# Attention and feed-forward: the first chunk's softmax transposed on TensorE, and a new plan of the first stage

## The chip, the cores and the metric

One core of one Trainium2 chip. A time is the device time of one execution in microseconds (us). The kernel is launched once and holds both parts of the computation.

## What is computed

Sliding-window attention over 8 batches and 8 heads, with 576 positions of width 64, and then a feed-forward layer on the result. Heads 0 to 3 see the 32 last positions (plain), heads 4 to 7 every fourth of the last 128 (dilated).

```python
scores = scale * np.matmul(q, k.transpose(0, 1, 3, 2))
rel = pos[:, None] - pos[None, :]
mask_plain = (rel >= 0) & (rel < window)                                  # window = 32
mask_dil = (rel >= 0) & (rel < window * dilation) & (rel % dilation == 0) # dilation = 4
scores = np.where(masks[None, :, :, :], scores, -1000000000.0)
attn = np.exp(scores - np.max(scores, axis=-1, keepdims=True))
attn = attn / (np.sum(attn, axis=-1, keepdims=True) + 1e-09)
x = np.matmul(attn, v)           # then (batch, position) x (head, width): 4608 x 512
h = x @ w_in                     # 512 x 2048
g = 0.5 * h * (1.0 + erf(h * inv_sqrt2))
return g @ w_out                 # 2048 x 512
```

## The kernel before

The 4608 rows are worked on in 9 chunks of 512: chunk c is the first 512 positions of batch c, and the ninth holds the remaining 64 of every batch. Within a chunk the heads go in four pairs: pairs 0 and 1 are plain, 2 and 3 dilated.

The attention of a pair has these steps, which are also the names in the plan. `scores` (line 318): 64 small matmuls of q and k and, in chunks 0 and 1, two with the unit matrix that put the mask into the bank first. `low` (`lowest`): the maximum, on VectorE. `exp` (`softmax`): 8 activations on ScalarE. `sums` and `norm`: the reciprocal of the sums, and the product with it. `t`: the transpose of the softmax. `av`: its product with v. `x` (`xout`): ScalarE copies the result as the rounded high part of x, VectorE subtracts to get the low part.

The feed-forward layer has 16 weights f, each with 512 columns of w_in's and 512 of w_out's work. They lie in memory as 64-bit numbers, and VectorE and ScalarE split each into a high and a low part (`w_split`, from line 235, and `w_high`, line 261). A weight in the list `TWICE` is loaded a second time, shifted by two bytes (`w_load_mid`), which spares VectorE one shift and one combination (lines 244 and 246) for one short instruction (line 242). The first `HALVED` weights are split in two halves. `ffn_h` (line 533) is 12 matmuls for one f, three for each pair's x; then gelu, and g is split like x. `ffn_o` (line 548) is 12 matmuls that add to four banks.

The first stage, up to chunk 0's last product, holds chunk 0's attention, all weights, chunk 1's attention and chunk 0's feed-forward layer. Its order is made on the host by the class `Plan`: each step has costs for its engines, steps it comes after, buffers that it takes and gives back, and a rank; the step that can start earliest goes next. The result is one fixed order of instructions on each engine. `FIRST`, `BLOCK`, `FETCH` and `FETCH_BUSY` are the planner's idea of how TensorE's program is loaded. The order of the loads, all issued by SyncE, is written out in `ORDER`: q and Q are the q and k of chunk 0 and 1, v and V their v, w a weight, m its shifted copy, n a tiny transfer that waits for a pair's sums.

PSUM has eight banks. Chunk 0's scores are in banks 6 and 7 (pairs 0 and 1) and 4 and 5 (pairs 2 and 3), each pair in its half of the columns; its products with v go to banks 0 to 3. The buffer `b67` stands for banks 6 and 7: chunk 0 holds it from pair 0's scores to pair 1's `exp`, then chunk 1 uses it for two pairs at a time: scores, transposes, products with v, until their x is out. `h` stands for banks 4 and 5, which `ffn_h` uses in turn; `ffn_o` adds up in banks 0 to 3.

In chunk 0 the transposes are VectorE's (`turn`, line 419: 32x32 blocks), so that v is needed in blocks of 32 keys, in an array `v_0` of its own with 5 blocks. In chunk 1 TensorE transposes (`turn_pe`, line 431, four of 128x128), ScalarE copies the result out of PSUM (line 434), and `av_one` (line 445) multiplies 64 keys deep.

The steps after the first stage (chunks 1 to 8, with the next chunk's attention between) are in an order written out by hand.

Of the kernel before, what the change touches and what calls it, by code (L numbers as in the profile page):

```python
# [18 lines left out]
P = 128  # L19
N = 512  # L20
REST = S - N
NCH = B + 1
# [11 lines left out]
TWICE = (3, 5, 6, 7, 8, 10, 11, 12, 13, 14)  # L34

HALVED = 3
# [11 lines left out]
RANK = dict(att0=-6760, split=19680, high=-4520, gelu=-6180, o=3550, scores=(-7120, -6830), low=(-5340, -70, -2990,  # L48
            680), exp=(3250, 2670, 3780, 6310), norm=(9560, 7320, 1160, 2270), t=(4820, 2320, 2390, 3790),
            av=(-14470, -8190), x=(-12250, -3790, -5560, -9110), store=5000)  # L50
# [106 lines left out]
def attn_ffn(ctx: ExitStack, tc: tile.TileContext, qk, qk_lp, qk_ld, v_0, v, v_ld, w, outT):  # L157
# [133 lines left out]
    def load_v(s):  # L291

        yield {"DMA": 1.6 if s.c == 0 else 2.6}
        a, b = xs[s.c][s.p], xs[s.c][s.p + 1]
        if s.c == 0:
            t = wpool.tile([P, 2, NU + 1, 2 * D], F32, tag="w", name="v_0")
            src = v_0[s.p // 2]
        else:
            t = wpool.tile([P, 2, NU, 2, 2 * D], F32, tag="w", name="v_sb")
            src = v[s.c - 1, s.p // 2]  # L300
        nc.sync.dma_start(t, src)
        a.v, b.v = t[:, 0], t[:, 1]
        if s.c == 1:
            a.v, b.v = (x.rearrange("p u j d -> p (u j) d").rearrange("p (a r) d -> p a r d", a=2) for x in (a.v, b.v))
# [13 lines left out]
    def scores(s, bank):  # L318

        yield {"PE:132": 1.15}  # L320
        s.at = 0 if s.wide else s.p % 2 * NU * 2 * KB
# [105 lines left out]
    def turn_pe(s, bank):  # L427

        yield {"PE:8": 0.25}
        for i in range(NU):  # L430
            nc.tensor.transpose(ps[:, bank, i * P:(i + 1) * P], s.all[:, 2 * i:2 * i + 2].rearrange("p i k -> p (i k)"), diag.bitcast(F32))
# [4 lines left out]
    def av_one(s, bank):  # L436

        yield {"PE:128": 1.0}
        for a in range(2):
            for r in range(4):  # L440
                for k in range(2):
                    rows = slice(k * 64, k * 64 + 64)
                    c0 = s.p % 2 * 256 + (2 * r + a) * KB
                    for h in range(2):
                        nc.tensor.matmul(ps[h * D:(h + 1) * D, bank + k, c0:c0 + KB], s.v[rows, a, r, h * D:(h + 1) * D],
                                         s.t[rows, h, a, r * KB:(r + 1) * KB], start=True, stop=True)

    def av(s, px, u0=0):

        yield {"PE:156": 0.95}  # L450
        s.px = px
        if s.c == 0:
            tiles = s.t.rearrange("p i j b -> p (i j) b")
            for m in (1, 3, 0, 2, 4):
                for r in range(4):
                    rows = slice(32 * r, 32 * r + 32)
                    if m == 0 and first(s, r, 0):
                        continue
                    for h in range(2):
                        def mm(q, i, start=m == 1):  # L460
                            nc.tensor.matmul(px(r)[h * D:(h + 1) * D, q * KB:(q + i.stop - i.start) * KB if i.step is None else (q + 2) * KB],  # L461
                                             s.v[rows, m, h * D:(h + 1) * D], tiles[rows, i], start=start, stop=m == NU)
                        i = [2 * (h * NU + slot(s, u)) for u in range(NU)]
                        if m == 1 and first(s, r, 0):
                            if s.plain:
                                mm(0, slice(i[0], i[0] + 3, 2))
                            else:
                                mm(0, slice(i[0], i[0] + 1))
                                mm(1, slice(i[1], i[1] + 1), False)
                        elif m == 0:  # L470
                            mm(0, slice(i[0], i[0] + 1))
                        elif m == NU:
                            mm(NU - 1, slice(i[NU - 1] + 1, i[NU - 1] + 2))
                        else:
                            mm(m - 1, slice(i[m - 1] + 1, i[m - 1] + 3))
            return
# [21 lines left out]
    def xout(s, px):  # L498
# [8 lines left out]
        elif s.c == 1:  # L507
            px = ps[:, 6:8, s.p % 2 * 256:s.p % 2 * 256 + 256].rearrange("p k (r a n) -> p k r a n", r=4, a=2)
# [17 lines left out]
    def ffn_h(c, f, gs):  # L526
        yield {"PE:24": 2.73}
        bank = ps[:, 4 + f % 2]
        n = 0
        for cc in range(NC):  # L530
            x = xs[c][cc].x
            for t, xx in ((0, 0), (1, 0), (0, 1)):
                nc.tensor.matmul(bank, weights[f][:, t, cc * P:(cc + 1) * P], x[:, xx],  # L533
                                 start=n == 0, stop=n == 3 * NC - 1)
                n += 1
        yield {"ACT/gelu": 0.6}
# [100 lines left out]
    for p in range(NPAIR):  # L637
        s, k = xs[0][p], (0, p)
        rank, even = RANK["att0"] + 10 * p, p % 2 == 0
# [206 lines left out]
```

## Time and profile before

| | |
|---|---|
| three runs, median | 911.31 us (911.13 to 911.84) |
| the profiled execution, its own time | 910.51 us |
| its span in the profile | 908.4 us |
| granted TensorE clock, mean | 0.985 |
| TensorE (PE) matmuls busy | 873.2 us, 96% |
| weight loads on TensorE (PEld) | 718.9 us, 79% |
| VectorE (DVE) busy | 357.9 us, 39% |
| ScalarE (ACT) busy | 370.9 us, 41% |
| GpSimd (POOL) busy | 9.6 us, 1% |
| read from and written to HBM | 66.06 and 9.44 MB |

The span runs from the first to the last instruction of the profiled execution; its own time is 2.1 us more. Shares are averages over the whole span, and the change touches only the beginning of it, so rows of single stretches say more than the table. A row of a wait gives as its reason what came last before it; "issue" means that nothing that the profile shows was missing.

### The profile page before, as it was taken

The numbers are of one execution on the slowest core, as the hardware profiler recorded it, in microseconds if no ns is written. First come the engines' busy times: TensorE is split into PE (matmuls) and PEld (weight loads), VectorE is DVE, ScalarE is ACT, GpSimd is POOL, SyncE is SP. The second block draws the span as 40 slices with busy tenths as digits, with TensorE's granted clock in tenths as the row PEclk, the third lists the DMA queues.
The fourth block names the chain that finished last, engine by engine and source line by source line (L and its number), as shares of the span: only waits on it lengthen the run. The fifth ranks groups of instructions, "written<-read, shape, count | busy, mean of one in ns | idle before, by whom it ended". The sixth has DMA issues, their size and how long they took to land.

```text
span 908.4 us, 19090 instructions
## 1 busy us (share of the span) xinstructions
PE 873.2 (96%) x8408; PEld 718.9 (79%) x8408; DVE 357.9 (39%) x612; ACT 370.9 (41%) x1016; POOL 9.6 (1%) x48
## 2 busy tenths in 40 slices
PE   4569999999999999999999999999999999999998
PEld 3458887888888888888888888888888888888886
DVE  3699991462146214621263225421552155212020
ACT  5548442543245423632273327232543254414040
POOL 4000000000000000000000000000000000000000
PEclk9599999999999999999999999999999999999999
DMA  9964614200410032003300330024000330010001
GB/s 370 417 252 182 260 63 151 83 0 1 170 65 1 1 129 105 1 1 122 113 1 1 117 118 1 1 79 155 2 0 20 133 144 21 1 38 12 1 1 47
DMA packets 17075, 76.72 MB, mean 84 GB/s; under 512 B 1888, under 2 KB 2144, under 8 KB 12768
## 3 DMA queue, kind: packets, MB, share of 16 engines
q1 hardware_dynamic: 16992, 75.50, 22.3%
q8 instruction: 66, 1.08, 0.5%
q14 instruction: 17, 0.14, 0.0%
HBM read 66.06 MB, written 9.44 MB: 83 GB/s over the span
## 4 chain that ended last, share of the span: by engine, by line
PE 92%; DVE 3%; ACT 2%; issue 1%; DMA 1%; POOL 0%; SPq 0%; POOLq 0%; ACTq 0%
PE ps L548 42%; PE ps L533 42%; PE ps L339 3%; PE ps L491 3%; ACT sm L384 1%; PE ps L461 1%; PE ps L325 1%; DMA raw_qk<-qk 1%; DVE raw_w L250 1%; PE ps L483 0%; DVE x L522 0%; DVE raw_w L246 0%; DVE st L353 0%; DVE weight L256 0%; ACT x L519 0%
## 5 line engine op out<-in xcount | busy, mean ns | idle before, releaser
L533 PE MATMUL ps<-x,weight 128*128 128x512 f32 x1728 | 404.5, 392 | 4.2 <-ACT weight L261 4.2
L548 PE MATMUL ps<-g,weight 128*128 128x512 f32 x1728 | 402.3, 391 | 0.0
L533 PEld LDWEIGHTS ps<-x,weight 128*128 128x128 f32 x1728 | 324.5, 189 | 74.1 <-ACT weight L261 5.2
L548 PEld LDWEIGHTS ps<-g,weight 128*128 128x128 f32 x1728 | 322.7, 188 | 67.4 <-issue 0.2
L543 DVE TENSOR_TENSOR g<-gf,g 128x512 fp32r<-128x512 f32 x144 | 99.6, 691 | 386.3 <-ACT g L541 386.2
L538 ACT ACTIVATE gf<-ps 128x512 f32<-128x512 f32 x144 | 86.1, 598 | 330.2 <-PE ps L533 330.2
L541 ACT CAST g<-gf 128x512 fp32r<-128x512 f32 x144 | 89.4, 621 | 4.6
L384 ACT ACTIVATE sm<-sm,st 128x64 f32<-128x64 f32 (+1 forms) x224 | 74.9, 336 | 0.1
L522 DVE TENSOR_TENSOR x<-ps,x 128x512 fp32r<-128x512 f32 (+1 forms) x40 | 31.8, 812 | 93.0 <-ACT x L519 93.0
L214 ACT COPY o_sb<-ps 128x512 f32<-128x512 f32 (+1 forms) x35 | 20.3, 581 | 108.7 <-PE ps L548 103.2
L519 ACT CAST x<-ps 128x512 fp32r<-128x512 f32 (+1 forms) x40 | 29.5, 768 | 66.4 <-PE ps L491 40.6
L424 DVE STREAM_TRANSPOSE turned<-sm 32x256 f32<-32x256 f32 x104 | 45.4, 436 | 2.0
L384 ACT ACTIVATION_READ_ACCUMULATOR sm<-sm,st 128x1 f32 x224 | 42.1, 188 | 0.0
L339 PEld LDWEIGHTS ps<-raw_qk 64*32 64x32 f32 x2304 | 26.4, 114 | 10.5 <-issue 9.3
L339 PE MATMUL ps<-raw_qk 64*32 64x64 f32 (+1 forms) x2304 | 30.9, 245 | 3.5 <-issue 2.7
L491 PEld LDWEIGHTS ps<-turned,v_sb 64*64 64x64 f32 x1664 | 25.4, 135 | 4.6 <-issue 4.6
L491 PE MATMUL ps<-turned,v_sb 64*64 64x32 f32 x1664 | 26.9, 220 | 0.0
L261 ACT CAST weight<-raw_w 128x1024 fp32r<-128x1024 f32 (+1 forms) x19 | 18.8, 989 | 7.8 <-DVE raw_w L250 7.7
L419 DVE STREAM_TRANSPOSE turned<-sm 128x512 f32<-128x512 f32 x30 | 21.3, 711 | 0.9
L384 ACT ACTIVATE sm<-ps,st 128x64 f32<-128x64 f32 x64 | 19.0, 334 | 6.4 <-PE ps L339 4.6
L406 DVE TENSOR_TENSOR sm<-sm,st 128x512 f32<-128x512 f32 x30 | 20.7, 691 | 0.9
L256 DVE SCALAR_TENSOR_TENSOR weight<-raw_w,spare 128x1024 fp32r<-128x1024 uint32 (+1 forms) x19 | 20.1, 1058 | 0.9
(51 smaller groups left out, 230.9 us busy)
## 6 DMA issues: line engine op xcount, KB each, us to landing
raw_qk<-qk SPq DMA_DIRECT2D x32, 512.0 KB, 6.2
raw_w<-w SPq DMA_DIRECT2D x16, 1024.0 KB, 7.7
v_sb<-v SPq DMA_DIRECT2D x15, 1024.0 KB, 5.1
mid_w<-w SPq DMA_DIRECT2D x10, 1023.5 KB, 8.3
outT<-o_sb SPq DMA_DIRECT2D x35, 256.0 KB, 2.1
raw_qk<-qk_ld SPq DMA_DIRECT2D x2, 1024.0 KB, 7.0
v_wide<-v_ld SPq DMA_DIRECT2D x2, 768.0 KB, 5.8
v<-v SPq DMA_DIRECT2D x2, 640.0 KB, 11.3
```

Of the source, the lines that this page charges most:

```text
L339: nc.tensor.matmul(s.sc[32 * r:32 * r + 32, h, c0:c0 + s.nk], x[:, q0:q0 + 32], x[:, k0:k0 + s.nk], start=s.c > 1, stop=s.c > 1 or u == NU ...
L384: nc.scalar.activation(t, s.sc[:, i // NU, at:at + 2 * KB] if s.c < 2 else t, AF.Exp, bias=s.st[:, 0, i:i + 1], scale=SCALE if s.c < 2 els ...
L419: nc.vector.transpose(s.t.rearrange("p i j b -> p (i j b)"), s.all.rearrange("p i k -> p (i k)"))
L424: nc.vector.transpose(s.t[32 * to:32 * to + 32, :, r % 2], s.all[32 * r:32 * r + 32, :, j * KB:(j + 1) * KB])
L491: nc.tensor.matmul(px(r)[h * D:(h + 1) * D, u * KB:(u + 1) * KB], s.v[rows, u, j, h * D:(h + 1) * D], s.t[rows, h * NU + slot(s, u), j], s ...
L519: nc.scalar.copy(h, y)
L522: nc.vector.tensor_sub(l, y, h)
L533: nc.tensor.matmul(bank, weights[f][:, t, cc * P:(cc + 1) * P], x[:, xx], start=n == 0, stop=n == 3 * NC - 1)
L538: nc.scalar.activation(gf, bank, AF.Gelu)
L541: nc.scalar.copy(g[:, 0], gf)
L543: nc.vector.tensor_sub(g[:, 1], gf, g[:, 0])
L548: nc.tensor.matmul(ps[:, d], weights[f][:, t, DM + d * P:DM + (d + 1) * P], gs[f][:, u], start=f == 0 and n == 0, stop=f == NF - 1 and n == 2)
```

## The change

Chunk 0's attention now goes as chunk 1's does: TensorE transposes the softmax (`turn_pe`), the result is copied out of PSUM by ScalarE or by VectorE as the plan chooses, and `av_early` (the former `av_one`) multiplies 64 keys deep. v of chunk 0 has the layout of the other chunks (1024 KB for two pairs instead of 640). Each pair of chunk 0 has two banks of its own for scores, transposes and products (4 and 5, 0 and 1, 2 and 3, 6 and 7); `b67` is taken by pair 3 alone and given back when its x is out. The first product of weights 0 and 1 is done in two parts: 6 matmuls that need pairs 0 and 1, and the others. `TWICE` has 7 weights instead of 10, `HALVED` is 1 instead of 3, and the order of the loads and all ranks of the plan are new.

```diff
-TWICE = (3, 5, 6, 7, 8, 10, 11, 12, 13, 14)
-HALVED = 3
+TWICE = (3, 5, 6, 7, 9, 14, 15)
+HALVED = 1
-BLOCK, FIRST, FETCH, FETCH_BUSY = 256, 63, 4.2, 5.9
+BLOCK, FIRST, FETCH, FETCH_BUSY = 256, 66, 3.9, 6.1
+FIRST_X = 2
-KAPPA, AHEAD = 2e-05, 5
-ORDER = ("q0 q1 Q0 q2 v2 q3 Q1 m5 w2 v0 w0 w1 w3 w4 Q2 Q3 V0 V2 m3 w5 w7 m7 m6 m10 w6 m8 w9 w8 m11 w12 m13 w10 "
-         "m12 w11 w14 m14 w13 w15")
+KAPPA, AHEAD = 6.5e-05, 4
+ORDER = ("q0 w0 q1 v0 q2 q3 w1 v2 w2 Q0 m6 m3 Q1 w3 n1 m5 m9 w6 w4 Q2 w7 w5 Q3 V0 w8 m7 w9 w11 w12 w10 w13 V2 "
+         "w14 w15 m15 m14")
...
-    def turn_pe(s, bank):
+    def turn_pe(s):
         yield {"PE:8": 0.25}
+        bank = s.bank + (s.p % 2 if s.c else 0)
         for i in range(NU):
             nc.tensor.transpose(ps[:, bank, i * P:(i + 1) * P], ...)
-        yield {"ACT": 0.6}
+        e = yield {"ACT": 0.6, "DVE": 0.61}
         s.t = work.tile([P, 2, 2, P], F32, tag="sm", name="turned", bufs=7)
-        nc.scalar.copy(s.t.rearrange("p h a n -> p (h a n)"), ps[:, bank])
+        copy(e, s.t.rearrange("p h a n -> p (h a n)"), ps[:, bank])
...
-    def ffn_h(c, f, gs):
-        yield {"PE:24": 2.73}
+    def ffn_h_first(c, f, n):
+        yield {f"PE:{6 * n}": 0.68 * n}
+        ffn_h_part(c, f, range(n))
+
+    def ffn_h(c, f, gs, n=0):
+        yield {f"PE:{6 * (NC - n)}": 0.68 * (NC - n)}
+        ffn_h_part(c, f, range(n, NC))
...
-        plan.add(("scores",) + k, scores(s, 6 if p < 2 else 4), [("load",) + k] + ([("scores", 0, p - 1)] if p else []),
-                 ["b67"] if p == 0 else [], [], rank)
+        own = ["b67"] if p == NPAIR - 1 else []
+        plan.add(("scores",) + k, scores(s, (4, 0, 2, 6)[p]), [("load",) + k] + ([("scores", 0, p - 1)] if p else []), own, [], rank)
-        plan.add(("t",) + k, turn(s), [("norm",) + k], ["sm"], ["sm"], rank)
-        px = px_four(p, 0)
-        plan.add(("av",) + k, av(s, px[0]), ...)
-        plan.add(("x",) + k, xout(s, px[1]), [("av",) + k], ["xg"], [], rank)
+        plan.add(("t",) + k, turn_pe(s), [("norm",) + k], ["sm"], ["sm"], rank)
+        plan.add(("av",) + k, av_early(s), ...)
+        plan.add(("x",) + k, xout(s, None), [("av",) + k], ["xg"], own, rank)
...
+        n = FIRST_X if f < 2 else 0
+        there = [("wsplit", f, 0), ("whigh", f, 0)]
+        if n:
+            plan.add(("h first", f), ffn_h_first(0, f, n), [("x", 0, p) for p in range(n)] + there, ["h"], [], r + RANK["gelu"])
```

## Rows read from the trace of the kernel before

**Rows 1.** Busy time by stretch: us, engines (x instructions), clock, DMA share, GB/s.

```profile
0.00:8.26 8.26, 1.91 (x66) 1.45 (x66) 0.00 (x0) 2.29 (x5) 6.52 (x34) 1.00 0.78 283
8.26:40.42 32.16, 15.69 (x642) 12.86 (x642) 17.01 (x41) 18.20 (x102) 3.07 (x15) 0.72 1.02 418
40.42:78.12 37.70, 29.85 (x352) 23.05 (x352) 35.25 (x61) 24.38 (x71) 0.00 (x0) 0.88 0.63 244
78.12:149.42 71.30, 71.30 (x437) 59.08 (x438) 57.73 (x71) 33.96 (x59) 0.00 (x0) 1.00 0.38 144
149.42:908.41 758.99, 754.49 (x6913) 622.50 (x6911) 247.89 (x441) 292.03 (x782) 0.00 (x0) 1.00 0.15 55
```

**Rows 2.** TensorE in order of time: start, duration, [idle before and reason].

```profile
19.32 0.41 PE L339 MATMUL ps<-raw_qk 64*32 64x64 f32 x19
22.40 0.94 PE L339 MATMUL ps<-raw_qk 64*32 64x64 f32 x45 [2.67 <-issue]
23.26 1.72 PE L461 MATMUL ps<-turned,v 32*64 32x32 f32 x83
28.44 1.39 PE L461 MATMUL ps<-turned,v 32*64 32x64 f32 x73 [3.45 <-issue]
32.07 1.21 PE L461 MATMUL ps<-turned,v 32*64 32x64 f32 x55 [2.23 <-DVE x L522]
34.64 0.64 PE L461 MATMUL ps<-turned,v 32*64 32x64 f32 x21 [1.36 <-issue]
36.68 1.65 PE L461 MATMUL ps<-turned,v 32*64 32x32 f32 x80 [1.41 <-DVE x L522]
40.42 5.49 PE L533 MATMUL ps<-x,weight 128*128 128x512 f32 x12 [2.09 <-ACT weight L261]
```

**Rows 3.** DMA queues from 13 to 39.5 us: packets, MB, share.

```profile
q8 instruction: 5, 0.08, 1.2%
```

**Rows 4.** Busy time in two stretches at half clock (columns as above).

```profile
22.40:46.00 23.60, 13.05 (x371) 10.84 (x371) 14.37 (x32) 14.37 (x59) 0.00 (x0) 0.50 1.01 418
...
63.20:66.50 3.30, 3.30 (x132) 2.63 (x132) 2.20 (x3) 0.00 (x0) 0.00 (x0) 0.50 0.71 298
```

**Rows 5.** Waits of VectorE up to 40.42 us: sum, times, longest.

```profile
DVE x L522 <- ACT x L519: 7.9, 3, 5.3
DVE st L353 <- ACT sm L384: 5.5, 2, 4.3
```

**Rows 6.** Waits of TensorE, 40 to 150 us: sum, times, longest.

```profile
PE ps L325 <- DVE x L522: 4.7, 1, 4.7
PE ps L533 <- ACT weight L261: 4.2, 4, 2.1
PE ps L445 <- ACT turned L434: 1.0, 1, 1.0
```

**Rows 7.** End of the stage in order of time, VectorE and TensorE.

```profile
134.49 1.22 DVE L256 SCALAR_TENSOR_TENSOR weight<-raw_w,spare 128x1024 fp32r<-128x1024 uint32 x1
...
141.26 2.88 PE L533 MATMUL ps<-x,weight 128*128 128x512 f32 x12
...
143.98 5.60 PE L548 MATMUL ps<-g,weight 128*128 128x512 f32 x24
```

**Rows 8.** Groups up to 150 us: count, busy us, mean ns, idle before.

```profile
L445 PE MATMUL ps<-turned,v_sb 64*64 64x32 f32 x256 | 4.1, 220 | 1.0 <-ACT turned L434 1.0
...
L246 DVE SCALAR_TENSOR_TENSOR raw_w<-raw_w 128x1024 uint32<-128x1024 uint32 x3 | 3.7, 1221 | 0.0
L419 DVE STREAM_TRANSPOSE turned<-sm 128x512 f32<-128x512 f32 x4 | 2.8, 709 | 0.0
...
L431 PE MATMUL ps<-early,sm 128*128 128x128 f32 x16 | 2.4, 287 | 0.0
L434 ACT COPY turned<-ps 128x512 f32<-128x512 f32 x4 | 2.2, 591 | 0.2 <-PE ps L431 0.2
...
L519 ACT CAST x<-ps 128x256 fp32r<-128x256 f32 x4 | 2.0, 656 | 0.7 <-PE ps L445 0.7
```

More of the change, by code (lines that the diff above doesn't have):

```diff
@@ L291, in load_v @@
     def load_v(s):
[L293 to L304, printed above, removed]
+        yield {"DMA": 2.6}
+        t = wpool.tile([P, 2, NU, 2, 2 * D], F32, tag="w", name="v_sb")
+        nc.sync.dma_start(t, v[s.c, s.p // 2])
+        for i in range(2):
+            o = xs[s.c][s.p + i]
+            o.v = t[:, i] if s.c > 1 else t[:, i].rearrange("p u j d -> p (u j) d").rearrange("p (a r) d -> p a r d", a=2)
     def load_v_wide(s):
@@ L444, in av_one @@
                     for h in range(2):
-                        nc.tensor.matmul(ps[h * D:(h + 1) * D, bank + k, c0:c0 + KB], s.v[rows, a, r, h * D:(h + 1) * D],
+                        nc.tensor.matmul(ps[h * D:(h + 1) * D, s.bank + k, c0:c0 + KB], s.v[rows, a, r, h * D:(h + 1) * D],
                                          s.t[rows, h, a, r * KB:(r + 1) * KB], start=True, stop=True)
     def av(s, px, u0=0):
-        yield {"PE:156": 0.95}
+        yield {"PE:128": 1.0}
         s.px = px
[L452 to L476, printed above, removed]
         if s.wide:
@@ L522, in xout, with ffn_h_part @@
             nc.vector.tensor_sub(l, y, h)
-    def ffn_h(c, f, gs):
-        yield {"PE:24": 2.73}
+    def ffn_h_part(c, f, ccs):
         bank = ps[:, 4 + f % 2]
-        n = 0
-        for cc in range(NC):
+        n = 3 * ccs[0]
+        for cc in ccs:
             x = xs[c][cc].x
@@ L663, in attn_ffn @@
         plan.add(("norm",) + k, norm(s, "ACT"), [("sums",) + k], [], [], rank["norm"])
-        plan.add(("t",) + k, turn_pe(s, 6 + p % 2), [("norm",) + k] + ([] if even else [("first", ("t", 1, p - 1))]),
+        plan.add(("t",) + k, turn_pe(s), [("norm",) + k] + ([] if even else [("first", ("t", 1, p - 1))]),
                  ["sm"] + (["b67"] if even else []), ["sm"] + ([] if even else ["b67"]), rank["t"])
@@ L670, in attn_ffn @@
         r = 100 * f
-        plan.add(("h", f), ffn_h(0, f, gs), [("x", 0, p) for p in range(NPAIR)] + [("wsplit", f, 0), ("whigh", f, 0)] +
-                 ([("begun", ("h", f - 1))] if f else [("low", 0, 3)]), ["h", "go", "xg"], ["h", "go"], r + RANK["gelu"])
+        n = FIRST_X if f < 2 else 0
+        there = [("wsplit", f, 0), ("whigh", f, 0)]
+        if n:
+            plan.add(("h first", f), ffn_h_first(0, f, n), [("x", 0, p) for p in range(n)] + there, ["h"], [], r + RANK["gelu"])
+        plan.add(("h", f), ffn_h(0, f, gs, n), [("x", 0, p) for p in range(NPAIR)] + there +
+                 ([("h first", f)] if n else []) + ([("begun", ("h", f - 1))] if f else []),
+                 ["go", "xg"] if n else ["h", "go", "xg"], ["h", "go"], r + RANK["gelu"])
         plan.add(("o", f), ffn_o_all(f, gs), [("h", f)] + [(n, f, len(parts(f)) - 1) for n in ("wsplit", "whigh")] + ([("begun", ("o", f - 1))] if f else []), [], ["xg"], r + RANK["o"])
@@ L811 @@
     rest = np.concatenate([vl, np.zeros_like(vl)], 0)
-    v_all = np.concatenate([vs[1:], rest[None]], 0)
-    v1 = vc[1].reshape(NPAIR, 2, 4, 2, 2, 2 * KB, D).transpose(0, 4, 5, 3, 2, 1, 6).reshape(NPAIR, P, NU, 2, 2 * D)
-    v_all[0] = v1
-    v_all = v_all.reshape(B, 2, 2, P, NU, 2, 2 * D).transpose(0, 1, 3, 2, 4, 5, 6)
-    c0 = cv[0].reshape(NPAIR, 2, 4, 4, KB, D)
-    before = np.zeros_like(c0[:, :, :, :1])
-    before[:2, :, 1:, 0] = c0[:2, :, :3, 3]
-    c0 = np.concatenate([before, c0], 3)
-    v_0 = c0.transpose(0, 2, 4, 3, 1, 5).reshape(2, 2, P, NU + 1, 2 * D).transpose(0, 2, 1, 3, 4)
+    v_all = np.concatenate([vs, rest[None]], 0)
+    for c in range(2):
+        one = vc[c].reshape(NPAIR, 2, 4, 2, 2, 2 * KB, D).transpose(0, 4, 5, 3, 2, 1, 6)
+        v_all[c] = one.reshape(NPAIR, P, NU, 2, 2 * D)
+    v_all = v_all.reshape(NCH, 2, 2, P, NU, 2, 2 * D).transpose(0, 1, 3, 2, 4, 5, 6)
     dl = batches(ldv).reshape(hp // 2, 2, 4, 4, 3, KB, D)
@@ L834 @@
     arrays, args = {}, []
-    for name, a in (("qk", qk), ("qk_lp", qk_lp), ("qk_ld", qk_ld), ("v_0", v_0), ("v", v_all), ("v_ld", v_ld), ("w", w)):
+    for name, a in (("qk", qk), ("qk_lp", qk_lp), ("qk_ld", qk_ld), ("v", v_all), ("v_ld", v_ld), ("w", w)):
         a = np.ascontiguousarray(a)
```

27 lines of the change are left out of this document (15 added, 12 removed).

## The prediction

> **What bounds the kernel now.** I began with the busy times by stretch [rows 1]. From 149.42 us to the end TensorE is busy 754.49 of 758.99 us, and no line that runs there does other work after the change. So only the first stage can move the time: chunk 0 with its attention, the splitting of the 16 weights, the attention of chunk 1, and chunk 0's two products. From 78.12 to 149.42 TensorE is busy throughout. What can be won lies before 78.12: 6.35 us without work up to 8.26, 16.47 up to 40.42, where the first product of x with a weight starts, and 7.85 up to 78.12. Work on TensorE that starts earlier, or waits less, brings the end forward one for one as long as weights and data keep up.
>
> Next I read what held TensorE before 40.42, in its order of time [rows 2]. Three waits have "issue" as their reason: 2.67 us ahead of 22.40, 3.45 ahead of 28.44, 1.36 ahead of 34.64. Between them stand 45 + 83 = 128 matmuls, then 73 + 55 = 128. Every matmul has its own weight load (642 and 642 in [rows 1]), so these are blocks of 256 instructions, and they run to a beat: 28.44 - 22.40 = 6.04 us, 34.64 - 28.44 = 6.20. In the same stretch one queue carries instructions, 5 packets with 0.08 MB [rows 3], 16 KB each. I read this as TensorE's own program being fetched block by block, while data fill the DMA engines (share 1.01, [rows 4]). The data matter less here than the count: 66 + 642 = 708 matmuls stand before the first product with a weight, and the last 80 + 21 + 55 + 73 + 83 + 45 = 357 of them follow the wait at 22.40. So the block borders lie behind matmul 351, 479 and 607, and at equal steps back 223 and 95.
>
> The Trainium skill would have it otherwise: Runtime: NRT & Kernel Launch, section Instruction fetch mechanics, gives the same 16 KiB block of 256 instructions, but a TensorE buffer of 2048 instructions, and calls the crossing mostly hidden. The waits of 2.67 and 3.45 us disagree with the second half; what the rule would give is the third rival.
>
> Two more things are needed. TensorE runs at 0.50 of its clock, 1.2 GHz, from 22.40 to 46, and again for 3.3 us after its longest later wait [rows 4]. And VectorE, which splits the weights, is busy only 17.01 of the 32.16 us up to 40.42 [rows 1], mostly behind late results of ScalarE, 7.9 and 5.5 us [rows 5], which were late with the fetches. From 40.42 to 78.12 it is busy 35.25 of 37.70, and TensorE's waits from 40 us on [rows 6] are 4.7 us for a subtraction that frees chunk 1's score banks, 1.0 for copies, and 4.2 for weights, of which 2.1 ends at 40.42 itself. The last weight is split at 134.49 + 1.22 = 135.7 and used at 141.26 [rows 7], so VectorE has some 5.5 us in hand.
>
> **The change, part by part.** *Fewer instructions before the first product.* Before it now stand 4 x 66 matmuls of chunk 0's scores (66 is the first pair, [rows 1]), 312 with v (83 + 73 + 55 + 21 + 80 in [rows 2]), and 2 x 66 scores of chunk 1, which come early because two pairs shared banks 6 and 7 and gave them on. After the change chunk 0's last pair holds these banks until its x is out, so chunk 1's scores follow later. A pair's product with v takes 64 matmuls in the new form (256 for four, [rows 8]) and 4 transposes (16 for four). That is 4 x (66 + 64 + 4) = 536 against 708: 172 fewer, 1.3 blocks. With 6 or 12 matmuls of the early product between, the last pair's product covers about 478 to 548, just behind the border at 479.
>
> *When that border opens.* Scores of the second pair no longer wait for the first pair's maximum in the same banks, so matmul 95 (29 into the second pair) comes at about 8.6 us; it is gated by the second load of q and k, now behind a weight of 1 MB: 2.1 MB in all. The first 8.26 us moved 283 GB/s, 2.34 MB, and 0.418 MB a us follow [rows 1], so it lands at about 7.7. Taking 6.1 us a block, 223 opens at 14.7, 351 at 20.8, 479 at 27.0. The last load of q and k is the sixth DMA, at 4.2 MB or about 12.7 us, ahead of 14.7; v's second half is 6.3 MB, about 17.7, ahead of the third pair's product. The two larger v transfers, 1024 instead of 640 KB, add 0.77 MB, 1.8 us of DMA, and lie before neither border. Bounds for the block: without any fetch wait the data would set the pace, some 4 us earlier; with one more border, 6.1 later.
>
> *The last pair.* 64 matmuls at half clock take about 1.7 us (80 took 1.65, [rows 2]): 28.7. Its x is copied in two pieces of 0.656 us [rows 8]: 30.0. I take that as the start of the first product, against 40.42: 10.4 us earlier.
>
> *First product in two parts.* For weights 0 and 1, 6 of 12 matmuls need only pairs 0 and 1. Both can run in the fetch waits, 12 of them go in 143.98 - 141.26 = 2.72 us at full clock [rows 7]: 2.7 us of work. Where they come too early they block the in-order queue; that needs weight 0, which is now the second transfer (1.6 MB, about 6.4 us), and VectorE has the room.
>
> *Transposes.* VectorE loses 4 x 0.709 = 2.8 us. In place come 4 x 4 transposes on TensorE (2.4 us for 16, some hidden in fetch waits) and 4 copies out of PSUM at 0.591 us, 2.4 us in all, on ScalarE or VectorE. Products wait for these copies, since they reuse the same banks; for the fourth pair the copy falls ahead of 27.0, so I cost it at nothing; uncovered, it is about 1 us.
>
> *Weights.* Three weights less are loaded twice: 3 MB less DMA, 7.3 us that nobody waited for, and VectorE does the extra combination three times more: 3 x 1.221 = 3.7 us. Two weights fewer in halves saves a few short instructions; I count nothing, at most 2 us. Net on VectorE: +3.7 - 2.8 = +0.9, up to +3.3 with the copies on it.
>
> *The sum for TensorE.* From 40.42 to 149.42 are 109.0 us, 7.85 of them idle, so 101.15 busy. The first product at half clock took 5.49 for 2.72, so 2.8 of that is clock [rows 2]. To the busy part add chunk 1's two score pairs, which are now behind the start, 132 matmuls, 3.3 to 3.6 us [rows 4], and take off the 2.7 done early: 101.15 + 3.6 - 2.7 = 102.0 with the same clock loss. 30.0 + 102.0 = 132.0 plus idle. Of the old idle, the 2.1 for weights should go: VectorE has 15.15 idle us before, in which it can split the first two. The 4.7 at chunk 1's banks and the 1.0 for copies I keep, and add 0.8 for a fetch inside chunk 1's product with v: 6.5. The stage ends at 138.5 instead of 149.4: 10.9 us. Bounds: idle 0 gives 17.4; idle 14 gives 3.4.
>
> *The check by VectorE.* If only 4 of its 15.15 idle us stay, the last weight is ready at 135.7 - 11.1 + 0.9 to 3.3 = 125.5 to 127.9; from the start of its product to the stage's end are 149.42 - 141.26 = 8.2 us, so not before 133.7 to 136.1. That is under 138.5, but not by much.
>
> The profiled execution took 910.51 us, 2.1 over its span, and the median of the runs is 911.31. 910.5 - 10.9 = 899.6 for such an execution, **900.4** for the median.
>
> **Rivals.** *VectorE becomes the limit* (chance 0.17). It has more weight work and the same idle time, since its instructions stand in one fixed order and wait behind softmax pieces. Idle as before puts the last weight at 136.6 to 139.0 and the end at 144.8 to 147.2: 2.2 to 4.6 us won; with 2.5 us of it filled, 4.7 to 7.1. Time 904 to 909. For it speaks that it was 94% busy after 40.42; against it, that weight 0, so far the eleventh transfer (7.6 MB, 20.8 us by the same reckoning), is there 14 us sooner.
>
> *One more fetch wait* (0.10): a border on the path, or slower fetches: 6.1 less, 4.8 won, 906.5. The beat of 6.04 and 6.20 speaks against it.
>
> *The shorter program buys nothing* (0.05): the waits called issue are not fetches and stay where they are. Then the first product starts no sooner for it, and what stays is the 2.7 us of early product: 908.6. The spacing of 128 matmuls and the packets speak against it. By the rule of the Trainium skill named above this would be the case, since crossings would cost next to nothing.
>
> *The clock stays down, and the kernel is slower* (0.05). After the start at 30, TensorE meets gaps and keeps to 1.2 GHz. Each group of 12 matmuls then costs 5.49 for 2.72, 2.77 more. Beyond four such groups more than now, about 22 us at half clock from the start, the 10.9 are spent; six give 917. For it: the clock stayed at half for 23 us and fell again after a later wait. Against: it came back within 6 us of the first product.
>
> *Better than forecast* (0.05): idle under 2 us, 894 to 896.
>
> **How the numbers follow.** The forecast itself has 0.58, and its own range is 896 to 904 (idle 2 to 10). The range 895 to 908 takes in the first two rivals nearly whole and leaves out the slower one, the best one, the third and the tail of the first, under 2 in 10. A measurement of this kernel tells changes of about 0.2%, 1.8 us, from none: faster 0.88, within 0.05 (tail of the first rival, the third), slower 0.07.
>
> **What would show it.** The first product with all pairs starts at 29 to 32 us with the first half products before it; issue waits at matmul 223, 351 and 479, none at 607 before it; VectorE works on weight 0 before 10 us and is idle under 8 us up to 40; half clock ends before 37; TensorE idles 4 to 9 us after the start; the stage ends near 138.5, and everything after is unchanged. I am wrong if the first product starts after 34, if TensorE waits over 8 us for weights behind it, or if a wait at chunk 1's banks grows.

## The result, and the profile after

The changed kernel takes 899.15 us, median of 4 executions (898.48 to 902.65), against 911.22 (910.14 to 911.84) for the kernel before on the same chip: ratio 0.9877, 95% interval 0.9849 to 0.9904. One execution of a variant below, old_code_new_plan, took 1345.54 us with a granted clock of 0.62; that kernel's time and ratio go by its other three. The forecast was 900.4, range 895 to 908. The profiled execution is the longest of the four: 902.65 us, span 900.9. A second profile of the same kernel (the experiment after_again, below) took 898.51 with a span of 896.7, and is shown where the two differ.

Busy time of the changed kernel by stretch, with the columns of [rows 1]. The borders are the same events as there but one: the end of the quiet start, the first product with all pairs of x, the end of chunk 1's last scores, the start of chunk 1's first product, the end. In the kernel before, the third border (78.12) is where TensorE's last wait of the stage ended; here that wait ends at 73.54, and 77.23 is the end of the scores behind it.

```profile
0.00:8.30 8.30, 1.97 (x67) 1.58 (x67) 0.00 (x1) 2.29 (x5) 6.55 (x34) 1.00 0.79 312
8.30:32.61 24.31, 19.89 (x476) 16.11 (x476) 23.43 (x46) 15.54 (x74) 5.38 (x15) 1.00 1.02 418
32.61:77.23 44.62, 40.03 (x535) 31.07 (x527) 41.71 (x58) 30.89 (x77) 0.00 (x0) 0.96 0.85 332
77.23:139.04 61.81, 61.81 (x393) 51.10 (x389) 44.90 (x60) 36.24 (x84) 0.00 (x0) 0.98 0.24 86
139.04:900.90 761.86, 756.04 (x6913) 623.89 (x6911) 247.95 (x441) 292.06 (x782) 0.00 (x0) 1.00 0.16 54
```

Against [rows 1]: the second stretch is 24.31 us instead of 32.16, has 166 matmuls less (476 against 642), and has VectorE busy for 23.43 of it, against 17.01 of 32.16. From the first product on TensorE idles 44.62 - 40.03 = 4.59 us, against 7.85. The last stretch has the same matmuls as before (6913) and is 2.87 us longer.

TensorE of the changed kernel in order of time: start, duration, idle before and its reason.

```profile
14.25 1.09 PE L429 MATMUL ps<-early,sm 128*128 128x128 f32 x4 [1.32 <-DVE st L353]
...
17.33 1.93 PE L444 MATMUL ps<-turned,v_sb 64*64 64x32 f32 x64 [0.44 <-ACT turned L216]
...
21.10 2.05 PE L444 MATMUL ps<-turned,v_sb 64*64 64x32 f32 x64 [0.80 <-DVE turned L218]
...
25.14 1.09 PE L429 MATMUL ps<-early,sm 128*128 128x128 f32 x4 [0.39 <-DVE sm L403]
...
28.02 2.93 PE L506 MATMUL ps<-x,weight 128*128 128x512 f32 x6
30.88 1.81 PE L444 MATMUL ps<-turned,v_sb 64*64 64x32 f32 x64
32.61 3.01 PE L506 MATMUL ps<-x,weight 128*128 128x512 f32 x12
...
37.80 1.65 PE L506 MATMUL ps<-x,weight 128*128 128x512 f32 x6
...
73.54 0.80 PE L322 MATMUL ps<-early 128*128 128x256 f32 x2 [2.17 <-DVE x L496]
...
77.23 4.38 PE L506 MATMUL ps<-x,weight 128*128 128x512 f32 x12
...
145.53 0.85 PE L336 MATMUL ps<-raw_qk 64*32 64x64 f32 x64 [0.89 <-DMA raw_qk<-qk]
147.54 0.86 PE L336 MATMUL ps<-raw_qk 64*32 64x64 f32 x64 [1.16 <-DMA raw_qk<-qk]
```

The three waits with the reason "issue" of [rows 2], 7.48 us in all, are gone, and nothing of that length has come in their place: from its first matmul at 6.33 up to 32.61 every wait of TensorE is for a piece of the softmax (L353, L403), a copied transpose (L216, L218), a load of q and k (0.95 us ahead of 11.75) or a cast of ScalarE (L263, 0.52 ahead of 23.66), and none passes 1.4 us. L429 are the four transposes of one pair, L444 the 64 matmuls of its product with v. At 28.02 stand the 6 early matmuls of weight 0, ahead of the last pair's product at 30.88. They take 2.93 us; 6 of the same shape take 1.65 at 37.80. So this stretch still runs at half clock, although the clock column above says 1.00 there: a duration of one and the same instruction at two places is the safer witness. The first product with all pairs, 12 matmuls in 3.01 us at 32.61, is at full clock. Chunk 1 begins at 139.04 instead of 149.42.

Instruction fetches of the changed kernel from 13 to 39.5 us, as in [rows 3], and then from 12 to 41 us, for the kernel before and for the changed one:

```profile
q8 instruction: 3, 0.05, 0.8%
```

```profile
q8 instruction: 5, 0.08, 1.1%
```

```profile
q8 instruction: 5, 0.08, 1.2%
```

The three packets against five of [rows 3] are an effect of the window: one packet starts at 12.90 us and one at 39.66. As many blocks are fetched in either kernel, and at much the same times: by the packed traces the packets end at 14.55, 20.87, 26.91, 33.07 and 39.36 us before, and at 14.05, 20.09, 26.35, 32.43 and 40.69 after. What differs is how many of them TensorE needs. Before, the three issue waits of [rows 2] end 1.53, 1.53 and 1.57 us behind the second, third and fourth packet. After, TensorE gets to the borders behind matmuls 223, 351 and 479 at about 16.0, 21.6 and 30.9 us (an estimate, counted along its order), 2.0, 1.5 and 4.5 us behind the end of the first, second and third packet, and the first product needs no fourth.

In the next row stands what VectorE waited for up to 40.42 us (sum, times, longest); [rows 5] had 7.9 and 5.5:

```profile
DVE x L496 <- ACT x L493: 1.2, 2, 1.0
```

And TensorE's waits from 40 to 150 us, as in [rows 6]:

```profile
PE ps L322 <- DVE x L496: 2.2, 1, 2.2
PE ps L336 <- DMA raw_qk<-qk: 2.1, 2, 1.2
...
```

The 4.7 us at chunk 1's score banks have become 2.2; the 4.2 for weights are gone. The 2.1 us for q and k fall at 145 to 148 us, behind the stage.

### The profile page after: what moved, and what is told of

Its sections match the earlier page's. It is cut to its first block, busy times and chain, and to the rows that moved or that the text cites. A ratio compares the mean times of both kernels' runs of the same rounds, so it can differ in the third digit from the quotient of the medians.

```text
span 900.9 us, 18988 instructions
## 1 busy us (share of the span) xinstructions
PE 879.7 (98%) x8368; PEld 723.8 (80%) x8368; DVE 358.0 (40%) x604; ACT 377.0 (42%) x1021; POOL 11.9 (1%) x48
## 4 chain that ended last, share of the span: by engine, by line
PE 91%; DVE 6%; DMA 1%; issue 1%; ACT 1%; POOL 0%; SPq 0%; POOLq 0%; ACTq 0%
PE ps L530 43%; PE ps L506 42%; PE ps L465 3%; PE ps L336 3%; DVE raw_w L252 1%; DVE weight L258 1%; DMA raw_qk<-qk 1%; PE ps L444 1%; DVE spare L254 1%; DVE spare L250 1%; DVE raw_w L248 1%; PE ps L457 0%; DVE st L350 0%; DVE g L525 0%; DVE x L496 0%
## 5 line engine op out<-in xcount | busy, mean ns | idle before, releaser
L216 ACT COPY o_sb<-ps 128x512 f32<-128x512 f32 (+1 forms) x35 | 20.4, 582 | 108.9 <-PE ps L530 103.2
L403 DVE TENSOR_TENSOR sm<-sm,st 128x512 f32<-128x512 f32 x30 | 20.7, 691 | 0.9
L263 ACT CAST weight<-raw_w 128x1024 fp32r<-128x1024 f32 (+1 forms) x17 | 18.5, 1096 | 3.8 <-DVE raw_w L252 3.8
L252 DVE SCALAR_TENSOR_TENSOR raw_w<-raw_w,spare 128x1024 uint32<-128x1024 uint32 (+1 forms) x17 | 19.8, 1167 | 0.5
```

The lines of the kernel that those rows point to most:

```text
L252: nc.vector.scalar_tensor_tensor(top, top, 0xC0000000, t, op0=ALU.bitwise_and, op1=ALU.bitwise_or)
```

## The experiments

Two theories stood against each other. F: the time comes from the shorter TensorE program, which reaches the first product with one or two fetched blocks less. V: it comes from VectorE, which gets weight 0 early and no longer stands idle; the fetches are then not what sets the start.

**old_code_new_plan.** The old attention code with the new constants, ranks and order of loads, so with 80-matmul products with v, but with weight 0 second.

```diff
-TWICE = (3, 5, 6, 7, 8, 10, 11, 12, 13, 14)
-HALVED = 3
+TWICE = (3, 5, 6, 7, 9, 14, 15)
+HALVED = 1
...
-ORDER = ("q0 q1 Q0 q2 v2 q3 Q1 m5 w2 v0 w0 w1 ...
+ORDER = ("q0 w0 q1 v0 q2 q3 w1 v2 w2 Q0 m6 m3 Q1 ...
```

> The attention of chunk 0 as before (transposes on VectorE, 32 keys deep, shared banks), with the load order, the ranks and the lists of weights of the changed kernel. Theory F (what counted before is the number of TensorE instructions ahead of the first product, fetched block by block): 708 matmuls still stand ahead of it, so it starts no earlier than about 38 us and at most 4 us of the gain stay, 907 to 914 us. Theory V (what counted is that VectorE gets weight 0 as the second transfer): most of the gain stays, 900 to 904 us.

Measured: 915.24 us against 911.05, ratio 1.0049 (1.0031 to 1.0066). It meets neither theory's number, F's by 1.2 us, and V alone falls: the early weight with the old code is slower than before. TensorE of this kernel:

```profile
30.47 0.63 PE L463 MATMUL ps<-turned,v 32*64 32x64 f32 x18 [2.89 <-issue]
34.41 1.63 PE L463 MATMUL ps<-turned,v 32*64 32x32 f32 x80 [3.31 <-DVE turned L421]
...
40.53 0.87 PE L341 MATMUL ps<-raw_qk 64*32 64x64 f32 x37 [3.17 <-issue]
...
43.17 7.38 PE L535 MATMUL ps<-x,weight 128*128 128x512 f32 x24
```

Issue waits of 2.89 and 3.17 us are still there (and one of 0.38 at 17.36), the last product with v waits another 3.31 for VectorE's transposes, and the first product starts at 43.17, later than before.

**new_code_old_plan.** The reverse: the new attention code, with its 64-matmul products, banks and early half products, and before's constants.

```diff
-TWICE = (3, 5, 6, 7, 9, 14, 15)
-HALVED = 1
+TWICE = (3, 5, 6, 7, 8, 10, 11, 12, 13, 14)
+HALVED = 3
...
-ORDER = ("q0 w0 q1 v0 q2 q3 w1 v2 w2 Q0 m6 m3 Q1 ...
+ORDER = ("q0 q1 Q0 q2 v2 q3 Q1 m5 w2 v0 w0 w1 ...
```

> The new attention of chunk 0 with the load order, the ranks and the lists of weights of the kernel before (first product in two parts kept). F: 172 matmuls less ahead of the first product, which starts near 32 us; 900 to 905 us. V: weight 0 is the eleventh transfer again and lands near 21 us, VectorE stands idle for some 12 us before, and the time is 908 to 914 us or more.

Measured: 918.71, ratio 1.0081 (1.0066 to 1.0096). F's number is missed, V's is met (its "or more"). TensorE of this kernel:

```profile
14.88 0.90 PE L335 MATMUL ps<-raw_qk 64*32 64x64 f32 x41 [1.54 <-issue]
...
24.24 3.42 PE L443 MATMUL ps<-turned,v_sb 64*64 64x32 f32 x119 [0.72 <-issue]
...
30.42 1.91 PE L443 MATMUL ps<-turned,v_sb 64*64 64x32 f32 x59 [0.51 <-issue]
...
37.90 3.38 PE L505 MATMUL ps<-x,weight 128*128 128x512 f32 x12
44.40 4.53 PE L505 MATMUL ps<-x,weight 128*128 128x512 f32 x12 [3.12 <-ACT weight L262]
...
120.20 8.12 PE L505 MATMUL ps<-x,weight 128*128 128x512 f32 x24 [6.00 <-ACT weight L262]
```

The mechanism under F is visible all the same. Here TensorE does reach the borders before the blocks, and waits at the places counted ahead of the chip: the first issue wait stands 23 matmuls into the fourth pair's 64 score matmuls, at 3 x 66 + 2 + 23 = 223, and ends at 14.88 (forecast 14.7). Chunk 0's attention is over at 30.42 + 1.91 = 32.3 instead of 38.3, and the first product starts 2.5 us sooner. But VectorE is busy only 12.23 of the 21.70 us from 8.3 to 30, and TensorE then waits 3.12 and 6.00 us for weights. The trace puts both down to order. The cast that ends the first wait stood on ScalarE behind eight activations of chunk 1's softmax, although VectorE's piece for it was done at 39.81. The cast that ends the second waited for a piece of VectorE that stood behind a subtraction for chunk 1's x, with VectorE idle for 5.50 us.

**before_scores1_late.** The kernel before, with one part of the new plan: chunk 1's scores come after chunk 0's last x, so that 132 matmuls less stand before the attention's end. To keep the buffers free, the loads for chunk 1 and some shifted copies move back in `ORDER` and `AHEAD` goes from 5 to 4 (not shown in the cut).

```diff
-        plan.add(("exp",) + k, softmax(s), ..., [], ["b67"] if p == 1 else [], rank)
+        plan.add(("exp",) + k, softmax(s), ..., [], [], rank)
...
-        plan.add(("x",) + k, xout(s, px[1]), [("av",) + k], ["xg"], [], rank)
+        plan.add(("x",) + k, xout(s, px[1]), [("av",) + k], ["xg"], ["b67"] if p == NPAIR - 1 else [], rank)
```

> The kernel before, with banks 6 and 7 given on only when x of chunk 0's last pair is out, so that chunk 1's first two pairs of scores (132 matmuls) come behind chunk 0's attention; the loads for chunk 1 and two shifted copies move back in the order to keep the buffers free. F: one block border less ahead of the first product, which starts 5 to 6 us earlier (near 35 us); time 904 to 907 us if the rest follows, since VectorE is fed as before and may hold part of it. V: VectorE gets no weight sooner, so within 2 us of before, or slower because chunk 1 comes later.

Measured: 911.61, ratio 1.0004 (0.9994 to 1.0013): no difference. TensorE:

```profile
31.41 1.65 PE L461 MATMUL ps<-turned,v 32*64 32x32 f32 x80 [1.41 <-DVE x L522]
...
38.00 3.85 PE L533 MATMUL ps<-x,weight 128*128 128x512 f32 x12
...
53.54 4.80 PE L548 MATMUL ps<-g,weight 128*128 128x512 f32 x12 [7.74 <-ACT g L541]
```

About one block less, and the last product with v starts 36.68 - 31.41 = 5.3 us sooner, as F has it. The start of the first product gains only 2.4, since the moved scores and the weight are still to come, and a wait of 7.74 us at 53.54 takes that back. That wait isn't V's: the product whose g is waited for was done at 41.85, but on ScalarE 16 activations of chunk 1's softmax stood ahead of the gelu; they waited for a maximum of VectorE until 45.53, and the gelu came at 52.23. So F gives an earlier start, and the order of the other engines decides what it is worth.

**before_av_twice.** More matmuls in front, nothing else: the products with v of two pairs of chunk 0 are done twice, 156 matmuls more, everything else as before.

```diff
-            for m in (1, 3, 0, 2, 4):
+            for m in (1, 3, 0, 2, 4) * (2 if s.plain else 1):
```

> The kernel before, with the products with v of chunk 0's pairs 0 and 1 done twice over into the same places (156 matmuls more, results the same). F: 1.2 blocks more ahead of the first product, which starts 6 to 7.5 us later, with one more wait for issue of 3 us or so; 916 to 919 us. Rival (the waits called issue are not fetches, only work counts): 156 matmuls at 1.65/80 us are 3.2 us, part of it inside waits; 911 to 914 us.

Measured: 920.42, ratio 1.0097 (1.0082 to 1.0112), 9.4 us more: nearer to F than to its rival, and 1.4 above F's range. TensorE:

```profile
22.40 0.69 PE L339 MATMUL ps<-raw_qk 64*32 64x64 f32 x45 [2.08 <-issue]
23.02 1.44 PE L461 MATMUL ps<-turned,v 32*64 32x32 f32 x83
28.43 2.27 PE L461 MATMUL ps<-turned,v 32*64 32x64 f32 x128 [3.97 <-issue]
34.63 0.64 PE L461 MATMUL ps<-turned,v 32*64 32x64 f32 x21 [3.93 <-issue]
37.52 1.94 PE L461 MATMUL ps<-turned,v 32*64 32x64 f32 x107 [2.25 <-DVE x L522]
40.56 0.95 PE L461 MATMUL ps<-turned,v 32*64 32x64 f32 x45 [1.09 <-issue]
...
46.64 5.01 PE L533 MATMUL ps<-x,weight 128*128 128x512 f32 x12 [2.08 <-ACT weight L261]
```

The waits of [rows 2] come at the same times although other matmuls stand there, again 128 apart (45 + 83, 128, 21 + 107), with steps of 6.03, 6.20 and 5.93 us, and there is one more, at 40.56. The first product starts 46.64 - 40.42 = 6.22 us later, one step. Issue waits behind 22.40 make 4.18 of it (3.97 + 3.93 + 1.09 against 3.45 + 1.36); the other waits are as before, and the rest, 2.04, is time in which TensorE works. The waits end 1.67, 1.45, 1.28 and 1.30 us behind the end of an instruction packet (20.73, 26.98, 33.35 and 39.26 us in the packed trace). That settles that the waits belong to the count of instructions and their fetches, not to data. The Trainium skill, in Runtime: NRT & Kernel Launch, section Instruction fetch mechanics, calls such crossings mostly hidden. The waits of 3.97 and 3.93 us disagree, here where the DMA engines are full.

**after_w0_late.** The changed kernel, with weights 0 and 1 behind all of q, k and v of chunk 0: V's part taken back, the code left alone.

```diff
-ORDER = ("q0 w0 q1 v0 q2 q3 w1 v2 w2 Q0 ...
+ORDER = ("q0 q1 v0 q2 q3 v2 w0 w1 w2 Q0 ...
```

> The changed kernel with weight 0 as the seventh transfer instead of the second (q and k and v of chunk 0 first). Theory V (VectorE sets the pace of the start, and must have a weight to split early): VectorE idles some 4 to 6 us up to 20 us and the time rises by 3 to 6 us, 902 to 905 us. Theory F alone (instruction blocks set the pace): at most 1 us more.

Measured: 903.67, ratio 0.992 (0.9905 to 0.9935), so 4.5 us above the changed kernel's median (3.9 by the two ratios), as V has it. Busy time of this kernel, and then of the changed one, from 8.3 to 20 us:

```profile
8.30:20.00 11.70, 8.03 (x267) 6.48 (x268) 6.85 (x19) 8.59 (x57) 3.03 (x15) 0.74 1.02 422
```

```profile
8.30:20.00 11.70, 8.98 (x270) 7.46 (x270) 11.32 (x27) 8.20 (x49) 5.38 (x15) 1.00 1.01 416
```

VectorE (third pair of numbers) is busy 6.85 us instead of 11.32. TensorE's start isn't worse for it: the first product starts at 29.86, sooner than in the changed kernel, since no half product stands ahead of the last pair here (after_first_moved below has 29.72). So V's number is met, but not because VectorE set the start. The fetches are back in sight, 2.88 us ahead of 15.16 and 0.56 ahead of 28.00, close to the forecast openings of 14.7 and 27.0. What is lost is lost later, in waits for weights, g and chunk 1's softmax up to 61 us, 2.66 the longest, and at half clock: the first product takes 5.10 us (3.01 in the changed kernel).

**before_late_w0.** Both shifts on the old code: chunk 1's scores late, by the two lines of before_scores1_late, and weight 0 second, with before's ranks.

```diff
-ORDER = ("q0 q1 Q0 q2 v2 q3 Q1 m5 w2 v0 w0 w1 ...
+ORDER = ("q0 w0 q1 v0 q2 q3 w1 v2 w2 Q0 m5 Q1 ...
```

> The attention of the kernel before, with chunk 1's first scores held back behind chunk 0's attention, and with weight 0 as the second transfer: both of the causes at once, without the new form of the products and without its ranks. If the two causes are all it takes: first product near 34 us, VectorE busy from 9 us on, 903 to 907 us. If the order of the rest, searched for the new form, is needed as well: the attention is early but the time is 909 us or more, with long waits of TensorE behind 40 us.

Measured: 917.78, ratio 1.0079 (1.0064 to 1.0094). The first product starts at 38.82, 1.6 us sooner than before, and then TensorE waits 9.41 us for a g of ScalarE at 54.23. The two ingredients together don't win with ranks made for another schedule.

**after_no_first.** The changed kernel without the half products, the rest of the plan worked out again from the same ranks.

```diff
-FIRST_X = 2
+FIRST_X = 0
```

> The changed kernel without the two half products (the first product of weights 0 and 1 in one part); the plan orders the rest anew. In the changed kernel 6 matmuls of the first half product stand ahead of the last pair's product with v and take 2.93 us at half clock. Theory F: they fill a wait, so without them the last pair's product starts no sooner, and 2.7 us of work move behind it: 901 to 904 us. Rival Q (they only stand in the way in the in-order queue): last pair's product 2 to 3 us sooner, time within 1 us of the changed kernel or less.

Measured: 905.41, ratio 0.9944 (0.9929 to 0.9959). It looks like 6 us for the half products, but the first product starts sooner, at 29.72; the loss is one wait, and half clock behind it (0.50 granted from 51.2 to 58.0 us), in an order that came out differently:

```profile
54.06 1.89 PE L429 MATMUL ps<-early,sm 128*128 128x128 f32 x4 [6.98 <-ACT sm L400]
```

**after_first_moved.** To take the order out of it: the same order, but all 12 matmuls of weights 0 and 1 are issued where the second half stood.

```diff
     def ffn_h_first(c, f, n):
         yield {f"PE:{6 * n}": 0.68 * n}
-        ffn_h_part(c, f, range(n))
...
         yield {f"PE:{6 * (NC - n)}": 0.68 * (NC - n)}
-        ffn_h_part(c, f, range(n, NC))
+        ffn_h_part(c, f, range(NC))
```

> The changed kernel in the very same order, except that the two half products are not done at their place but at that of the other half (12 matmuls at once). The run without half products had another order and a wait of 6.98 us that the changed kernel does not have; this run keeps the order. Theory Q (they stand ahead of the last pair's product with v and gain little): the last pair's product starts 2 to 3 us sooner and the whole is within 1 us of the changed kernel. Theory F (they fill a wait): 2 to 3 us more than the changed kernel.

Measured: 899.2, ratio 0.9874 (0.986 to 0.9889), against 898.53 for the changed kernel beside it. The first product starts at 29.72, and the stage ends at 136.65 instead of 135.99. The two kernels differ by 0.67 us, within the interval. So the half products are worth under 1 us, and the 6 us of the run before were the order's.

**after_less_vector.** The changed kernel with 5.3 us less work on VectorE: the shift and the combination for the low part of weights 1, 2 and 4 are left out.

```diff
-            nc.vector.tensor_scalar(low, low, 9, None, op0=ALU.logical_shift_right)
+            if f not in (1, 2, 4):
+                nc.vector.tensor_scalar(low, low, 9, None, op0=ALU.logical_shift_right)
...
-            nc.vector.scalar_tensor_tensor(low, top, 23, low, op0=ALU.logical_shift_left, op1=ALU.bitwise_or)
+            if f not in (1, 2, 4):
+                nc.vector.scalar_tensor_tensor(low, top, 23, low, op0=ALU.logical_shift_left, op1=ALU.bitwise_or)
```

> The changed kernel, same order, without the shift and the combination that make the low part of weights 1, 2 and 4 (left out of the computation; VectorE has 3 x 1.8 = 5.3 us less to do between 19 and 48 us). Theory V: VectorE set the pace there, TensorE's waits between 32 and 74 us (4.6 us in sum) shrink and the first products come sooner; 894 to 897 us. Rival T (TensorE, fetches or the data order set the pace): within 1 us of the changed kernel.

Measured: 898.61, ratio 0.9868 (0.9852 to 0.9884), half a microsecond below the changed kernel's 899.15, no difference beyond the interval. V's gain isn't there. VectorE is busy 9.09 of 12.60 us from 20 to 32.6 (12.11 in the changed kernel), and the first product starts only 0.85 us sooner, at 31.76. The wait at chunk 1's banks is unchanged:

```profile
72.39 0.50 PE L324 MATMUL ps<-early 128*128 128x256 f32 x2 [2.17 <-DVE x L498]
```

It is one of order. VectorE of the changed kernel, in order of time:

```profile
69.74 0.69 DVE L525 TENSOR_TENSOR g<-gf,g 128x512 fp32r<-128x512 f32 x1
70.35 0.69 DVE L250 TENSOR_SCALAR spare<-raw_w 128x1024 uint32<-128x1024 uint32 x1
71.07 1.23 DVE L252 SCALAR_TENSOR_TENSOR raw_w<-raw_w,spare 128x1024 uint32<-128x1024 uint32 x1
72.21 1.28 DVE L496 TENSOR_TENSOR x<-ps,x 128x512 fp32r<-128x512 f32 x2
```

ScalarE's part of x is done at 68.66 + 1.11 = 69.77, and the subtraction stands behind three instructions until 72.21. Here VectorE is 93% busy (41.71 of 44.62 us behind the first product) without its load being the limit: what counts is what stands in front of the instruction that is waited for.

**after_again and after_early_load_again.** The changed kernel profiled a second time, and beside it a version that loads q and k of chunk 2 at the end of the first stage, once weight 15's splitting has begun (after_early_load was the first run of that version: 897.51, ratio 0.9857, 0.9842 to 0.9871).

```diff
+    for i in range(NPAIR):
+        dma(("load", 2, i), load(xs[2][i]), ["w"] if i % 2 == 0 else [], [("first", ("wsplit", NF - 1, 0))])
...
-            add(c, (3.25 + .25 * (p % 2)) if wide else (-32 if c == 1 else 0) + A_QK - 32 + .25 * p if c > 1 else 0, 0, load(s[p]))
+            if n > 2:
+                add(c, (3.25 + .25 * (p % 2)) if wide else A_QK - 32 + .25 * p, 0, load(s[p]))
```

> The changed kernel with q and k of chunk 2 loaded at the end of the first stage, once the last weight has begun to be split, instead of behind the stores of chunk 0. In the profile of the changed kernel TensorE waits 0.89 and 1.16 us for these loads at 145 to 148 us, and runs at half clock for 3.4 us after, 1.7 us of loss. Theory B (this border takes back part of the gain): 2 to 3.7 us less than the changed kernel, 895 to 897 us. Rival: the waits are only in that one profile, or the scores wait for something else next; within 1 us.

> The changed kernel itself, for a second profile beside the first (whose execution took 902.65 us where the others took 898.5 to 899.6). If the two half-clock stretches of the first profile (from 73.4 and from 148.5 us) are what makes that execution longer, this one lacks at least one of them and its span is 3 to 4 us shorter; the first stage then ends at 136 to 138 us. If they are always there, span near 901 us.

> The changed kernel with q and k of chunk 2 loaded at the end of the first stage, once more with more rounds beside the changed kernel. Theory B: the waits at the border of chunk 1 (2.0 us in the first profile) go, 1.5 to 3 us less than the changed kernel. Rival: no difference beyond the interval.

Measured: after_again 898.53 (898.04 to 899.72), ratio 0.987 (0.9854 to 0.9887); after_early_load_again 896.0 (895.31 to 897.23), ratio 0.9841 (0.9827 to 0.9856). The second profile lacks both half-clock stretches of the first, and its span is 4.2 us shorter. The early load is 2.5 us faster than the changed kernel run beside it, the fastest version here. TensorE of after_again, then of after_early_load_again:

```profile
73.11 0.50 PE L322 MATMUL ps<-early 128*128 128x256 f32 x2 [2.20 <-DVE x L496]
...
75.55 3.01 PE L506 MATMUL ps<-x,weight 128*128 128x512 f32 x12
...
135.99 5.60 PE L506 MATMUL ps<-x,weight 128*128 128x512 f32 x24
142.38 0.85 PE L336 MATMUL ps<-raw_qk 64*32 64x64 f32 x64 [0.79 <-DMA raw_qk<-qk]
143.57 0.86 PE L336 MATMUL ps<-raw_qk 64*32 64x64 f32 x64 [0.34 <-DMA raw_qk<-qk]
```

```profile
141.87 1.48 PE L336 MATMUL ps<-raw_qk 64*32 64x64 f32 x128
143.28 5.73 PE L506 MATMUL ps<-x,weight 128*128 128x512 f32 x24
```

With the early load the scores of chunk 2 run without a wait, and TensorE is busy 21.00 of the 21.00 us from 139 to 160, where the changed kernel is busy 18.95 in the first profile and 18.63 in the second. Only 0.79 + 0.34 of the second's idle time are waits for the loads; 1.23 is an issue wait ahead of 152.69, which the early load hasn't got. Why it is gone too, these runs don't show.

## Why the prediction was right

The total came out: 900.4 forecast, 899.15 measured, inside the narrower range of 896 to 904 too. The mechanism holds in its main part, and three of its terms were mis-sized in opposite directions: against the second profile the start was forecast 2.2 us too early, the time from there to the stage's end 4.7 too long and the rest 1.7 too short. That they cancel to about a microsecond is luck. Side by side, with both profiles of the changed kernel:

| us | forecast | first profile | after_again |
|---|---|---|---|
| first product with all pairs starts | 30.0 | 32.61 | 32.18 |
| from there to the stage's end | 108.5 | 106.43 | 103.81 |
| idle in that | 6.5 | 4.59 | 4.58 |
| stage ends | 138.5 | 139.04 | 135.99 |
| rest of the span | 759.0 | 761.86 | 760.71 |
| execution | 899.6 | 902.65 | 898.51 |

*Fewer instructions before the first product, and the border count*: right. The blocks come as before, but the first product needs none later than the one that begins at 479; no issue wait stands ahead of it, and where TensorE arrives in time it waits at matmul 223 (new_code_old_plan, after_w0_late). In before_av_twice 156 matmuls more put the first product off by 6.22 us, 4.18 of it in issue waits. That the waits would be seen at 223, 351 and 479 in the changed kernel was wrong: there TensorE comes to every border after the block has landed.

*When that border opens* and *The last pair*: the start was 2.6 us too early, and not for the reason feared. The fourth pair's product began at 30.88 instead of 27.0. Its transposes came at 25.14: the chain back from there is VectorE's without a break from 8.30 to 25.00, pieces of the softmax between pieces of weights 0 and 1 (VectorE was busy 23.43 of 24.31 us); and the half product stood in front of it with 2.93 us. Without that half product (after_first_moved) the product follows at once and the first product starts at 29.72, within the forecast.

*First product in two parts*: the step that failed. "Both can run in the fetch waits, 12 of them ... 2.7 us of work": only 6 of them ran ahead, not in a wait but on the path, at half clock. The gain is under 1 us (898.53 against 899.2), not 2.7.

*Transposes*: the copies out of PSUM cost little, as forecast; waits for them are 0.44 and 0.80 us.

*The sum for TensorE*: 102.0 busy was forecast "with the same clock loss" of 2.8. In after_again there is none after the start (granted clock 1.00 from 31.5 to 895), and TensorE is busy 99.23 from 32.18 on: 102.0 - 2.8 for the clock, + 1.4 for the 6 matmuls that weren't early, - 1.3 for chunk 1's scores, which took 2.3 us at full clock instead of 3.6, gives 99.3. Idle was 4.59 where 6.5 stood: the wait for chunk 1's banks shrank from 4.7 to 2.2, and the fetch I had added there for 0.8 didn't show.

*Everything after is unchanged*: nearly. The tail is 2.87 us longer in the first profile, with 0.89 + 1.16 = 2.05 us of waits for chunk 2's loads, where before had 0.88, and a stretch at half clock behind them; and 1.72 longer in after_again, with 0.79 + 0.34 of these waits and an issue wait of 1.23 at 152.69.

Why did the first profile take 4 us more than the second? Busy time of the changed kernel in two stretches of the first one:

```profile
73.40:80.20 6.80, 6.66 (x139) 5.29 (x140) 6.66 (x9) 0.28 (x1) 0.00 (x0) 0.50 0.47 157
...
148.50:151.90 3.40, 3.40 (x9) 2.63 (x10) 0.00 (x0) 0.00 (x0) 0.00 (x0) 0.50 1.00 400
```

Both follow a wait, 2.17 us ahead of 73.54 and 1.16 ahead of 147.54. The same 12 matmuls take 4.38 us at 77.23 and 3.01 in the second profile; that stage ends 3.05 later, 0.43 of it from the start. The same wait (2.20 us) in the second profile does not lower the clock. Why it does in one execution and not in the other, these runs don't show.

Of the rivals, *VectorE becomes the limit* comes nearest: it paces the start as part of a chain. But with 5.3 us of its work left out, 3.0 of it ahead of 32.6, the kernel gains 0.5, so that load isn't the limit; the splitting of weight 0 itself was left in. *The shorter program buys nothing* falls with before_av_twice in one direction, and holds in another: on the old schedule an attention that ends 5.3 us sooner bought nothing (before_scores1_late). My sum let an earlier start of TensorE "bring the end forward one for one as long as weights and data keep up". That condition is what the mixed kernels fail. Either half of the change alone gives 915 to 919, and late scores with the early weight on the old code 917.78.

Open: how much of these losses is the order alone. None of the mixed kernels had its ranks searched for, so they bound the parts from one side, and a share of the 12 us can't be given to code and plan separately. That a long product with v in the searched order would still win was not tried.

## What to carry to other kernels

Count the instructions of an engine up to the point that matters when waits with no visible cause come at a fixed step while the DMA queues are full, each just behind a packet of the instruction queue; the count says where the next one will be. Choose a window around such packets with care, since one at its edge drops out. But an earlier start of one engine is worth only what the in-order queues of the others let through: before costing a busy engine by its load, look at what stands in front of the one instruction that is waited for. And a part that is put in or taken out under a plan made for something else measures the plan; keep the order fixed, as after_first_moved did, before giving a part the credit.

## What the runs showed of the hardware that was not expected

The step of about 6 us is not always kept: in new_code_old_plan the second block opened 9.36 us after the first (14.88 to 24.24), the third 6.18 after that. TensorE stood in other waits there, but so it did in the changed kernel, where the packets end 6.04, 6.26 and 6.08 us apart. What starts a fetch stays open.

Half clock costs small matmuls less than large ones: the 64 score matmuls of a pair take 1.19 us at half clock (74.27 in the first profile) and 0.86 at full (73.54 in the second); 12 products of x with a weight take 5.49 (40.42 in [rows 2]) against 3.01.

The clock column reads 1.00 up to the first change that a profile records: 18.8 us in the kernel before, 32.4 in the changed one. The durations say otherwise. The 64 score matmuls take 1.19 us from 7.04 on in both, the half-clock time, so half clock covers more of the start than [rows 4] shows.
